# V and its ones columns stored at a pitch of 200 columns instead of 194

## Chip, cores, metric

One core of one Trainium2 chip. The metric is device time in microseconds (us) of one execution.

## The reference

Two branches share one normalised input: sliding-block attention over the last 512 keys of a cache (32 heads of 192), and a gated feed-forward net. Only the attention matters here (condensed; xn is the normalised input):

```python
W = min(4096, max(256, Sk // 4))                      # 512 keys
q = (xn @ wq).reshape(B, Sq, Hq, Dh).transpose(0, 2, 1, 3)
v = v_cache[:, :, Sk - W:, :]
p = softmax(einsum("bhqd,bhkd->bhqk", q, k) * Dh ** -0.5)
o = einsum("bhqk,bhkd->bhqd", p, v)                   # the product that reads V
...
return x + (o_rows @ wo) * silu(ffn(xn))
```

Sizes: 2048 queries, model width 640, Dh = 192, bf16.

## The kernel before

V of two heads lies in one tile: 128 keys on the partitions, then 4 key chunks (kc), 2 heads (h), and 192 columns of V followed by two columns of ones. The product with the unnormalised softmax weights reads 193 of these columns, so that column 192 of the result is the sum of the weights, by which `divide` divides.

```python
V_p = consts.tile([P, KC, 2, Dh + 2], bf, name="V_p")          # pitch 194 columns, 388 bytes
...
nc.gpsimd.memset(V_p[:, :, :, Dh : Dh + 2], 1.0)               # once
...
def load_v(pr):                                                # L121, once for each pair of heads
    for h in range(2):
        nc.sync.dma_start(out=V_p[:, :, h, 0:Dh], in_=vv[2 * pr + h, k0:Sk, :]. ... )
...
# in pv, line 487, for all pairs of heads but the last two: two row tiles of 64 keys, side by side
for kc in range(KC):
    for n, r in enumerate((lo, hi)):
        ...
        m = nc.tensor.matmul(
            acc[:, k, h * 256 : h * 256 + Dh + 1],
            Ps[i][kc][r, h, qt * P : (qt + 1) * P], V_p[r, kc, h, 0 : Dh + 1], ...)
...
# in pv_full, line 539, the last two pairs: all 128 keys at once
nc.tensor.matmul(acc[:, k, h * 256 : h * 256 + Dh + 1],
                 Ps[i][kc][:, h, qt * P : (qt + 1) * P], V_p[:, kc, h, 0 : Dh + 1], ...)
```

A "slice" below is one (kc, h) of V_p, the moving operand of one such matmul. `Ps`, the stationary operand, is the p_t of the profile. The slices are read in the order h=0, kc 0 to 3, then h=1, kc 0 to 3. (In L487 the two row tiles of a slice start mostly 19 or 20 ns apart and run side by side; they are called a pair, and count once.)

The softmax here doesn't subtract the row's maximum and nothing guards it: scores larger than these inputs give would overflow.

## Time and profile before

| | before |
|---|---|
| time, median of 3 runs | 920.98 us (920.84 to 921.37) |
| span of the profiled run | 919.1 us |
| TensorE busy | 914.2 us, 99% |
| next busiest engine (VectorE) | 601.8 us, 65% |
| matmuls that read V_p | L487: 3584 (1792 pairs); L539: 256 |

The lines themselves stand in the prediction. The gaps from start to start on which it rests come from the single start times in the trace's records; a timeline, which merges neighbours, shows only sums of such gaps. The ends of matmuls, and so their durations, are modelled in this profile and not measured.

The view of the instructions that touch V_p gives durations as minimum/median/maximum:

```profile
L487 PE MATMUL mm<-V_p,p_t x3520: 241/242/244, 190.4 to 817.2; 64*128 64x193 bf16 x196
L539 PE MATMUL mm<-V_p,p_t x224: 244/246/258, 841.3 to 900.4; 128*128 128x193 bf16 x112
```

### The profile page before, as it was taken

To read this page: it belongs to the slowest core of one execution; us is meant where nothing else is said; L and a number is where in the kernel's file an instruction comes from. 1 tells how busy PE (TensorE), PEld (TensorE's weight loads), DVE (VectorE), ACT (ScalarE), POOL (GpSimd) and SP (SyncE) were. 2 spreads that over 40 slices of the span, in tenths; PEclk is the share of its full clock that TensorE was granted. 3 is DMA by queue.
4 is the path that set the end of the run, shared out by engine and by line. 5 is a ranking of instruction groups with operands and counts; after the bars stand their busy time and mean duration, and the time that the engine had idled before them with its cause. 6 is when DMAs were issued, how large, how long until landed. Compare 5 with 4: busy or idle time off the path is not lost.

```text
span 919.1 us, 23174 instructions
## 1 busy us (share of the span) xinstructions
PE 914.2 (99%) x9920; PEld 548.9 (60%) x9920; DVE 601.8 (65%) x844; ACT 473.9 (52%) x840; POOL 85.2 (9%) x269
## 2 busy tenths in 40 slices
PE   9999999999999999999999999999999999999998
PEld 6444444465757575656565656566666666665665
DVE  6443321467677777777777777676867777777657
ACT  4222222557464646565656565655555555556471
POOL 0000000000000000000000000000000000001976
PEclk9999999999999999999999999999999999999999
DMA  9412430045352534253534343435243444443525
GB/s 299 79 35 64 92 82 0 1 75 112 54 113 50 111 51 108 54 108 54 108 58 109 57 108 52 110 53 108 56 87 73 90 77 75 91 71 102 120 59 166
DMA packets 248167, 77.53 MB, mean 84 GB/s; under 512 B 228993, under 2 KB 248065, under 8 KB 248065
## 3 DMA queue, kind: packets, MB, share of 16 engines
q1 hardware_dynamic: 245696, 73.39, 38.9%
q10 hardware_dynamic: 2368, 2.67, 0.9%
q8 instruction: 77, 1.26, 0.6%
q14 instruction: 26, 0.20, 0.1%
HBM read 38.93 MB, written 2.62 MB: 45 GB/s over the span
## 4 chain that ended last, share of the span: by engine, by line
PE 99%; DMA 1%; DVE 0%; ACTq 0%; issue 0%
PE mm L448 22%; PE sc L462 18%; PE mm L487 16%; PE sc L602 15%; PE sc L282 11%; PE mm L312 6%; PE sc L572 4%; PE sc L564 2%; PE mm L539 2%; PE mm L564 1%; DMA x_t<-in_A_x_dram 1%; PE gu L282 0%; PE mm L321 0%; PE sc L487 0%; PE sc L539 0%; PE mm L462 0%
## 5 line engine op out<-in xcount | busy, mean ns | idle before, releaser
L466 ACT ACTIVATE p_t<-sc 128x1024 bf16<-128x1024 f32 x254 | 252.9, 1022 | 120.5 <-PE sc L462 120.5
L453 DVE TENSOR_REDUCE qT<-mm 128x512 bf16<-128x1024 f32 x189 | 231.1, 1223 | 99.0 <-PE mm L448 96.5
L517 ACT ACTIVATE O_b<-mm,r 128x192 bf16<-128x192 f32 x486 | 164.6, 421 | 183.7 <-issue 136.9
L448 PE MATMUL mm<-xnT,wq_p 64*128 64x512 bf16 x1890 | 237.5, 376 | 0.0
L462 PE MATMUL sc<-qT,khat 64*128 64x512 bf16 x1524 | 198.0, 376 | 0.0
L487 PEld LDWEIGHTS <-p_t 64*128 64x128 bf16 x3584 | 159.3, 93 | 33.8
L487 PE MATMUL mm<-V_p,p_t 64*128 64x193 bf16 x3520 | 176.7, 242 | 0.0
L615 DVE TENSOR_TENSOR s_m<-s_m,sc 128x1024 f32<-128x1024 f32 x108 | 131.9, 1221 | 60.7 <-PE sc L602 52.3
L602 PE MATMUL sc<-wo_p,OT_b 64*128 64x512 bf16 x1296 | 168.8, 376 | 0.0
L448 PEld LDWEIGHTS <-wq_p 64*128 64x128 bf16 x1890 | 105.0, 94 | 98.9 <-issue 0.8
L462 PEld LDWEIGHTS <-khat 64*128 64x128 bf16 x1536 | 85.3, 94 | 80.4 <-DVE s_t L615 0.3
L602 PEld LDWEIGHTS <-OT_b 64*128 64x128 bf16 x1296 | 70.1, 94 | 44.1 <-issue 0.3
L615 DVE TENSOR_TENSOR s_t<-s_t,sc 128x512 f32<-128x512 f32 x108 | 74.2, 687 | 28.4 <-PE sc L572 26.6
L589 POOL MEMSET turn_t<- 128x1 f32 x220 | 21.6, 98 | 700.2 <-PE mm L487 506.2
L290 DVE TENSOR_TENSOR hT<-sc,sg 128x512 bf16<-128x512 f32 x46 | 31.7, 692 | 81.5 <-ACT sg L289 81.5
L289 ACT ACTIVATE sg<-sc 128x512 bf16<-128x512 f32 x46 | 27.3, 596 | 69.8 <-PE sc L282 69.8
L282 PE MATMUL sc<-xnT,wu_sb 128*128 128x512 bf16 (+1 forms) x260 | 60.5, 355 | 0.0
L282 PE MATMUL sc<-xnT,wg_sb 128*128 128x512 bf16 (+1 forms) x260 | 60.3, 355 | 0.1
L572 PE MATMUL sc<-OT_b,wo_p 64*128 64x512 bf16 (+1 forms) x345 | 50.3, 376 | 0.0
L312 PE MATMUL mm<-wd_sb,hT 128*128 128x512 bf16 x192 | 43.9, 379 | 0.0
L282 PEld LDWEIGHTS <-wu_sb 128*128 128x128 bf16 x285 | 27.2, 98 | 26.8 <-issue 0.2
L282 PEld LDWEIGHTS <-wg_sb 128*128 128x128 bf16 x285 | 27.2, 98 | 26.3
(83 smaller groups left out, 418.8 us busy)
## 6 DMA issues: line engine op xcount, KB each, us to landing
wo_p<-in_A_wo_dram SPq DMA_DIRECT2D x16, 480.0 KB, 4.8
K_p<-in_A_k_cache_dram SPq DMA_DIRECT2D x32, 192.0 KB, 4.6
V_p<-in_A_v_cache_dram SPq DMA_DIRECT2D x32, 192.0 KB, 3.6
wq_p<-in_A_wq_dram SPq DMA_DIRECT2D x64, 80.0 KB, 2.9
wq_p<-in_A_wq_dram SPq DMA_DIRECT2D x16, 160.0 KB, 3.2
x_t<-in_A_x_dram SPq DMA_DIRECT2D x13, 160.0 KB, 3.2
x_b<-in_A_x_dram SPq DMA_DIRECT2D x4, 512.0 KB, 6.4
OT_b<-O_b SPq DMA_TRANSPOSE x124, 2.8
```

Source lines behind the costliest of these rows:

```text
L282: nc.tensor.matmul(out, w_sb[:, c, f * P : (f + 1) * P], xnT[:, c, qc], start=(c == 0), stop=(c == NC - 1),)
L290: nc.vector.tensor_tensor(hTs[b][:, f, :], u, sg[:], ALU.mult)
L312: nc.tensor.matmul(dn, at, by, start=(f == 0), stop=(f == NF - 1))
L448: nc.tensor.matmul(q_ps[:, h, :], pairs[pr]["wq"][r, c, j * P : (j + 1) * P], xnT[r, c, b * 512 : (b + 1) * 512], start=(c == 0), stop=(c ...
L453: nc.vector.reduce_sum(qTs[i][:, j, :], q_ps[:, :, :].rearrange("p h n -> p n h"), axis=AX.X)
L462: nc.tensor.matmul(sc[:, h, :], khat[r, j, ks], qT[r, j, :], start=(j == 0), stop=(j == 2))
L466: nc.scalar.activation(p_t[:, :, :], sc[:, :, :], ACT.Exp, scale=scale)
L487: m = nc.tensor.matmul(acc[:, k, h * 256 : h * 256 + Dh + 1], Ps[i][kc][r, h, qt * P : (qt + 1) * P], V_p[r, kc, h, 0 : Dh + 1], start=(p ...
L517: nc.scalar.activation(O_b[:, qt, h, :], a_k[:, h, 0:Dh], ACT.Copy, scale=r[:, k, h, :])
L572: nc.tensor.matmul(ps.rearrange("p (t q) -> p t q", q=P), pairs[i // NB]["wo"][r, j, MC:D], OTs[i][:, :, :].rearrange("p (t j) q -> p j t ...
L602: m = nc.tensor.matmul(ps[:, k, :], OTs[i][r, 3 * (2 * half + k) + j, :], pairs[i // NB]["wo"][r, j, MAIN], start=(turn == 0 and j == 0), ...
L615: nc.vector.tensor_tensor(to, to, ps, ALU.add)
```

## The change

The intent: 194 columns are 388 bytes, so slices begin at 0, 4, 8 or 12 bytes past a multiple of 16. With 200 columns, 400 bytes, each begins at a multiple of 16. It was hoped that TensorE would then read V faster.

```diff
-    V_p = consts.tile([P, KC, 2, Dh + 2], bf, name="V_p")
+    V_p = consts.tile([P, KC, 2, Dh + 8], bf, name="V_p")
```

What else moves with it is told in the prediction.

## The prediction

> **What bounds the kernel now.** I read the page from the top: busy shares, then the chain that ended last, then the costliest groups, then the DMA issues.
>
> ```profile
> PE 914.2 (99%) x9920; PEld 548.9 (60%) x9920; DVE 601.8 (65%) x844; ACT 473.9 (52%) x840; POOL 85.2 (9%) x269
> ...
> PE 99%; DMA 1%; DVE 0%; ACTq 0%; issue 0%
> ```
>
> Only TensorE matters: it is busy 914.2 of 919.1 us and makes up 99% of the chain; the next engine is at 65%. The granted clock is 9 tenths or more in all 40 slices. Whatever shortens the stream of matmuls shortens the kernel by as much, and a change elsewhere must first use up a third of the span.
>
> ```profile
> L448 PE MATMUL mm<-xnT,wq_p 64*128 64x512 bf16 x1890 | 237.5, 376 | 0.0
> L487 PEld LDWEIGHTS <-p_t 64*128 64x128 bf16 x3584 | 159.3, 93 | 33.8
> L487 PE MATMUL mm<-V_p,p_t 64*128 64x193 bf16 x3520 | 176.7, 242 | 0.0
> ...
> V_p<-in_A_v_cache_dram SPq DMA_DIRECT2D x32, 192.0 KB, 3.6
> ```
>
> These are groups and one DMA row of the page. The number after the bar is busy time, then the mean of one, then idle time before it. V_p is read by L487 only as the moving operand (193 columns: 192 of V and one of ones), and no idle time stands before it. The same groups with shapes kept apart show the other reader of V_p, the last pair of heads:
>
> ```profile
> L539 PE MATMUL mm<-V_p,p_t 128*128 128x193 bf16 x224 | 20.8, 246 | 0.0
> ...
> L539 PE MATMUL sc<-V_p,p_t 128*128 128x193 bf16 x32 | 2.8, 246 | 0.0
> ```
>
> The duration of one matmul (242 ns) is not its cost, as matmuls overlap. What each takes from the span is the time to the next start. The timeline of a stretch shows it:
>
> ```profile
> 515.25 0.85 PE L487 MATMUL mm<-V_p,p_t 64*128 64x193 bf16 x16
> 515.92 1.47 PE L602 MATMUL sc<-wo_p,OT_b 64*128 64x512 bf16 x12
> 517.22 0.85 PE L487 MATMUL mm<-V_p,p_t 64*128 64x193 bf16 x16
> ```
>
> The first column is the start. Sixteen matmuls of L487 take 515.92 - 515.25 = 0.67 us. They run in pairs, rows 0 to 63 beside rows 64 to 127, so that is 8 pairs at 84 ns. The twelve of L602 take 1.30 us, 6 pairs at 217 ns.
>
> The single start times in the trace's records are finer, and they decide this prediction. I took the gap from each L487 pair to whatever starts next and sorted the 1792 pairs by slice of V_p. With h the head and kc the key chunk, a slice starts at (2 kc + h) x 388 bytes. In the order of execution, mean gaps in ns are: h=0: 83.1, **85.8**, 82.5, 82.5; h=1: 82.5, **86.7**, 82.5, 82.5. Each is a mean over 224 pairs. The slow two are kc=1. They repeat to within 1 ns (85 or 86; 86 or 87), whatever rows of p_t are the weights and whatever stretch of the kernel. L539, not row-tiled and in another order of heads and query tiles, has the same pattern: 85.8 and 86.7 at kc=1, and 82.5 elsewhere except 83.5 for the first. The first slice's 83.1 comes from following a 512-column matmul (83.3 there, 82.5 after another L487), so it is not the address's.
>
> [...]
>
> **The change part by part.** No instruction is added, removed or reordered. Three things move.
>
> First, slice starts go from multiples of 388 bytes to multiples of 400. The kernel before, as built, has V_p at byte 16,896, a multiple of 64, and everything in front of it stays. Before, starts modulo 32 are 0, 8, 16, 24 for kc 0 to 3 of h=0 and 4, 12, 20, 28 for h=1: eight different values, of which 8 and 12 are slow. Afterwards they are 0 for all of h=0 and 16 for all of h=1. Both values occur before, at kc=0 and kc=2 of h=0, and both cost 82.5 ns. I chose the modulus 32: 16 fails, as 8 and 12 modulo 16 also occur at kc=3, which is fast. If the address causes the slow slices, then all pairs should take 82.5. The gain in L487 is 224 x (85.83 - 82.50) + 224 x (86.67 - 82.50) = 0.75 + 0.93 = 1.68 us. In L539, with 32 matmuls for each slice, it is 32 x (3.28 + 4.22) = 0.24 us. All of it lies on the path, as TensorE has nothing to wait for. Sum: -1.92 us, 0.2%.
>
> Second, V_p grows by 8 slices x 6 columns x 2 bytes = 96 bytes per partition, so every buffer placed behind it moves by 96 bytes: xnT, khat, qT, wq_p, p_t and OT_b from 32 to 0 modulo 64. [...]
>
> Third, the V loads write rows of 384 bytes at a 400-byte pitch, and the ones columns are set at another pitch, once. The 32 loads land in 3.6 us median; the table of waits has no wait of TensorE for V_p, so a faster or slower landing is hidden: 0. The set of ones is one 113 ns instruction at the very start: 0.
>
> Full effect: 920.98 - 1.92 = 919.06 us. My point value is a mixture of this and no gain, below.
>
> **The rivals.** *Nothing happens* (921.0 us). The slow slices come from the position in the sequence and not the address. For it: [...]the ends of matmuls are more even than their starts (durations 241 to 244 ns, longer just where the gap is longer), so the records may only shift a start within an even 83.5 ns pace. Against it: kc=2 is the same kind of matmul as kc=1, and h=0 and h=1 differ though the sequence is the same.
>
> *The new starts hit slow places* (922.9 us). Modulo 64 the new starts are 0, 16, 32 and 48; the last two don't occur before. If they are slow, four of eight slices cost some 3.75 ns extra instead of two, so 256 x 4 x 3.75 = 3.84 us of excess in place of 1.92. Nothing in the trace suggests it beyond two slow values out of eight.
>
> *Alignment frees more* (down to 914.6 us). If the whole overhead of V_p's matmuls were due to alignment they would go at 193/2.4 = 80.4 ns: 149.7 + 21.4 us of gaps now against 2048 x 80.4 = 164.7, 6.4 us less. Against it: the first slice, which starts at a multiple of 64 bytes already, costs 82.5, and 512-column matmuls from 32-byte-aligned buffers carry the same small overhead.
>
> *The 96-byte shift moves something else*, such as a transposing DMA or a ScalarE write. ScalarE and VectorE have 48% and 35% of the span free, so I allow 0.5 us either way.
>
> **Range and chances.** I give 0.55 to the full gain (919.1), 0.25 to nothing (921.0), 0.08 to slow places, 0.05 to more, and the rest to shifts. The mean is 919.7; I lean to the likeliest outcome and say 919.4. Three runs before lie within 0.5 us. The range is 918.5 to 921.4. Even the largest rival is 0.7%, so "within 2%" is nearly certain: 0.98, and 0.01 for each side.
>
> **What would show it.** Right: gaps of L487 pairs of 82.5 ns in all eight slices but for the first after a 512-column matmul, durations of L487 closer together than 241 to 244, L487 plus L539 taking 1.9 us less of the span, counts of instructions unchanged, and 512-column gaps still 215.8. Wrong at the first step: kc=1 still 3 to 4 ns slow, with the time at 921, or another slice slow. Wrong at the second: PV gaps as predicted but other groups changed. A new wait of TensorE for V_p, or a clock below full, would make the whole prediction wrong.

The forecast's sum is -1.92 us (1.68 in L487 and 0.24 in L539). One term of 0 is that for the buffers moved by 96 bytes; in the trace before, pairs of their 512-column matmuls start 215.7 to 216.0 ns apart (means of L448, L462 and L602).

The 2.4 in the rival "Alignment frees more" is columns per ns. The trace before shows it: in L564, 256 columns take 109.2 ns from start to start and 512 take 215.7, 0.416 ns for each further column. The 80.4 ns and the 914.6 us are an estimate from that price. The "small overhead" is 82.5 ns against 80.4, and 215.8 ns for 512 columns against 512/2.4 = 213.3.

## The result, and the profile after

| | before | after |
|---|---|---|
| time, median of 4 runs | 921.0 us (920.84 to 921.37) | 920.5 us (920.35 to 921.18) |
| ratio | | 0.9995, 95% interval 0.9978 to 1.0013 |
| span of the profiled run | 919.1 us | 919.1 us |

A ratio is always the mean time of one kernel's runs over that of the other's of the same rounds, so it isn't quite the ratio of the medians quoted.

The page of the kernel after, its engines and its chain:

```profile
PE 912.6 (99%) x9898; PEld 548.9 (60%) x9920; DVE 601.7 (65%) x844; ACT 474.4 (52%) x840; POOL 85.3 (9%) x269
...
PE 99%; DMA 1%; DVE 0%; ACTq 0%; issue 0%
```

The bound is unchanged. TensorE's 1.6 us less busy time is no gain: 22 matmul records are missing from this trace (9898 of 9920), all of them outside the groups that read V_p. (The repeat of this kernel, number 1 below, has all 9920 and shows 913.8 us.)

The V load did land faster, 3.3 us against 3.6 (but the K load, whose tile kept its pitch, also went from 4.6 to 4.4), and nobody waits for it:

```profile
V_p<-in_A_v_cache_dram SPq DMA_DIRECT2D x32, 192.0 KB, 3.3
```

The instructions that touch V_p, kernel after:

```profile
L487 PE MATMUL mm<-V_p,p_t x3520: 243/243/243, 190.6 to 817.2; 64*128 64x193 bf16 x196
L539 PE MATMUL mm<-V_p,p_t x224: 247/247/257, 841.3 to 900.4; 128*128 128x193 bf16 x112
```

All L487 durations are now the same, 243 ns. The gaps became as even, but not as the prediction had it. Mean gap in ns from the start of an L487 pair to the next start, by slice, from the start times in the records:

```
            h=0: kc 0   1     2     3     h=1: kc 0   1     2     3     sum of L487, us
before        83.12 85.83 82.50 82.50       82.50 86.67 82.50 82.50     149.66
after         83.35 83.32 83.33 83.35       83.32 83.33 83.35 83.32     149.33
```

The two slow slices lost 2.5 and 3.3 ns, and the others gained 0.8 ns, all but the first one. Every slice now costs 83.33 ns, or 200 clocks. (A clock here is 0.417 ns, the price of one more column in these traces: from 192 columns, 82.5 ns in number 6, to 512 columns, 215.8 ns, it is 133.3 ns for 320 columns. Turned round, it is the 2.4 GHz of a forecast below.) L487 gained 0.33 us and L539 0.04 us. L602 and L572, the matmuls after the last slices, took 0.09 and 0.05 us more. From the first L448 of the attention to the last matmul it is 748.26 us before and 748.05 us after: 0.2 us, where 1.9 was expected. (There is one trace of the kernel before. Number 2, which reads V_p in the same way, comes to within 0.03 us of its stretch, when its four stray gaps are taken off.)

The timeline of the stretch that the prediction showed, kernel after (start, length):

```profile
515.36 0.85 PE L487 MATMUL mm<-V_p,p_t 64*128 64x193 bf16 x16
516.02 1.47 PE L602 MATMUL sc<-wo_p,OT_b 64*128 64x512 bf16 x12
517.32 0.76 PE L487 MATMUL mm<-V_p,p_t 64*128 64x193 bf16 x14
```

Eight pairs take 516.02 - 515.36 = 0.66 us, against 0.67 before; at this resolution the change can't be seen.

Before this stretch lies the feed-forward net, up to the first L448. It took 167.03 us in the trace before and 167.23 after, and between 166.77 and 168.05 over all 14 traces. Those 1.3 us from start to start are larger than the whole effect, so the traces decide here and the times only bound it.

### The profile page after: what moved, and what is told of

Same layout as the page of the kernel before. It is cut to its first block, busy times and chain, and to the rows that moved or that the text cites. A ratio compares the mean times of both kernels' runs of the same rounds, so it can differ in the third digit from the quotient of the medians.

```text
span 919.1 us, 23152 instructions
## 1 busy us (share of the span) xinstructions
PE 912.6 (99%) x9898; PEld 548.9 (60%) x9920; DVE 601.7 (65%) x844; ACT 474.4 (52%) x840; POOL 85.3 (9%) x269
## 4 chain that ended last, share of the span: by engine, by line
PE 99%; DMA 1%; DVE 0%; ACTq 0%; issue 0%
PE mm L448 22%; PE sc L462 18%; PE mm L487 16%; PE sc L602 15%; PE sc L282 11%; PE mm L312 6%; PE sc L572 4%; PE sc L564 2%; PE mm L539 2%; PE mm L564 1%; DMA x_t<-in_A_x_dram 1%; PE gu L282 0%; PE mm L321 0%; PE sc L539 0%; PE sc L487 0%
## 5 line engine op out<-in xcount | busy, mean ns | idle before, releaser
L448 PE MATMUL mm<-xnT,wq_p 64*128 64x512 bf16 x1890 | 237.5, 376 | 0.0
L462 PE MATMUL sc<-qT,khat 64*128 64x512 bf16 x1524 | 198.0, 376 | 0.0
L487 PEld LDWEIGHTS <-p_t 64*128 64x128 bf16 x3584 | 159.0, 94 | 33.8
L487 PE MATMUL mm<-V_p,p_t 64*128 64x193 bf16 x3520 | 176.4, 243 | 0.0
L602 PE MATMUL sc<-wo_p,OT_b 64*128 64x512 bf16 x1296 | 168.9, 376 | 0.0
L448 PEld LDWEIGHTS <-wq_p 64*128 64x128 bf16 x1890 | 105.0, 94 | 98.9 <-issue 0.8
L462 PEld LDWEIGHTS <-khat 64*128 64x128 bf16 x1536 | 85.3, 94 | 80.4 <-DVE s_t L615 0.3
L602 PEld LDWEIGHTS <-OT_b 64*128 64x128 bf16 x1296 | 70.3, 94 | 44.1 <-issue 0.3
L572 PE MATMUL sc<-OT_b,wo_p 64*128 64x512 bf16 (+1 forms) x345 | 50.3, 376 | 0.0
```

The source lines that it names most:

```text
L448: nc.tensor.matmul(q_ps[:, h, :], pairs[pr]["wq"][r, c, j * P : (j + 1) * P], xnT[r, c, b * 512 : (b + 1) * 512], start=(c == 0), stop=(c ...
L462: nc.tensor.matmul(sc[:, h, :], khat[r, j, ks], qT[r, j, :], start=(j == 0), stop=(j == 2))
L487: m = nc.tensor.matmul(acc[:, k, h * 256 : h * 256 + Dh + 1], Ps[i][kc][r, h, qt * P : (qt + 1) * P], V_p[r, kc, h, 0 : Dh + 1], start=(p ...
L572: nc.tensor.matmul(ps.rearrange("p (t q) -> p t q", q=P), pairs[i // NB]["wo"][r, j, MC:D], OTs[i][:, :, :].rearrange("p (t j) q -> p j t ...
L602: m = nc.tensor.matmul(ps[:, k, :], OTs[i][r, 3 * (2 * half + k) + j, :], pairs[i // NB]["wo"][r, j, MAIN], start=(turn == 0 and j == 0), ...
```

## The experiments

What was open: why did the slices at 82.5 ns get slower when they were aligned? Three theories were set against each other.

- *Even pace*: a slice of 193 columns costs 200 clocks, 83.33 ns, wherever it starts. A different offset only shifts the recorded start of a matmul within that pace.
- *Slow places*, the prediction's: starts at 8 or 12 modulo 32 cost 3 to 4 ns more, the true cost elsewhere is 82.5 ns, and something else, such as the shift of the other buffers, gave the gain back.
- *Groups of eight*: the 200 clocks of the kernel after are also 25 x 8, so the price could go by groups of eight columns, 25 of them for 193 columns as for 200. This was a guess; nothing but that one number spoke for it.

Three batches of four kernels ran, each of five rounds with the kernel before on the same chip (medians of the kernel before 921.29, 921.04 and 921.25 us). The edits of numbers 2, 5 and 8 are shown against the kernel before, those of the others against the changed kernel. "Stretch" is the time from the first L448 to the first L539, from the start times: 674.28 us in the kernel before. It holds all 1792 pairs of L487 and excludes the unsteady beginning.

### 1. The changed kernel again

No edit.

> The changed kernel again, in five rounds. Even pace (each pair takes 200 clocks of 2.4 GHz, 83.33 ns, wherever its slice starts; the offset only shifts the recorded start): all eight slices 83.3 ns again, durations all 243 ns, and the whole 0.3 to 0.5 us below the kernel before, ratio 0.9995. Slow places removed but given back elsewhere: the same gaps, time anywhere within 0.5 us.

Measured: 921.03 us, ratio 0.9994 (0.9982 to 1.0007). Gaps of 83.3 ns in all slices, durations 243 ns, L487 149.34 us, stretch 674.10 us, as in the first trace of this kernel. The trace's numbers repeat to 0.01 us; the times can't tell the kernels apart.

### 2. The shift of the other buffers alone

```diff
     V_p = consts.tile([P, KC, 2, Dh + 2], bf, name="V_p")
+    pad_t = consts.tile([P, 48], bf, name="pad_t")
+    nc.gpsimd.memset(pad_t[:], 0.0)
```

> Pitch 194 as before, with a 96-byte tile behind V_p, so that all later buffers stand where the change puts them. Even pace: the pattern of before stays (85.8 and 86.7 ns at kc=1, 82.5 elsewhere), L487 gaps sum to 149.7 us, time as before, 921.0. If the shift of the other buffers is what slowed the 82.5 ns slices to 83.3 in the changed kernel: slices at 83.3 with kc=1 at 86.7 and 87.5, sum of L487 and L539 1.7 us more, time 922.7.

Measured: 922.09 us, ratio 1.0005 (0.9992 to 1.0017). The gaps are those of before: 85.85 and 86.69 ns at kc=1, 82.5 elsewhere, but for the first slice (83.0) and the last (84.06). The last's mean holds four single gaps of 149 to 216 ns, 0.35 us more than four of 82.5. Each of them ends 155 ns after GpSimd began to write `turn_t` (line 591 of this kernel), so TensorE seems to have waited for that write; the profile names it in one of the four, and why it happens in this build only is open. Without the excess L487 sums to 149.64 us, as before (149.66). So the shift alone did not slow the 82.5 ns slices; the new pattern came with the pitch. The median was 0.8 us above that of the kernel before, between the two forecasts, so the time alone would not have told them apart. In its trace, which is of a slower run (922.58 us), 1.0 us more than in the trace before lies ahead of the attention (168.05 us to the first L448), where V_p isn't read.

### 3. Pitch 200, every slice 8 bytes late

```diff
-                out=V_p[:, :, h, 0:Dh],
+                out=V_p[:, :, h, 4 : 4 + Dh],
-        nc.gpsimd.memset(V_p[:, :, :, Dh : Dh + 2], 1.0)
+        nc.gpsimd.memset(V_p[:, :, :, 4 + Dh : 6 + Dh], 1.0)
...            # and in both matmuls
-                        V_p[r, kc, h, 0 : Dh + 1]
+                        V_p[r, kc, h, 4 : Dh + 5]
```

> Pitch 200, but every slice starts 8 bytes into its 400 bytes, so at 8 modulo 16 (8 modulo 32 for h=0, 24 for h=1). Even pace: flat 83.3 ns, sum of L487 149.3 us, time as the changed kernel, 920.5. A start at 8 modulo 32 costs 85.8 ns (the prediction's reading): h=0 at 85.8, h=1 at 82.5, sum over 2048 matmuls 172.4 us against 170.7 of the changed kernel, time 922.2.

Measured: 921.17 us, ratio 0.9999 (0.9986 to 1.0011). Flat 83.3 ns, durations 243 ns, L487 149.34 us, stretch 674.10 us: the numbers of the changed kernel, with no slice at a multiple of 16 bytes. The slow place at 8 modulo 32 is refuted: h=0 starts there in every slice and is not slow. The other one, 12, isn't tried here; in number 8 the slice h=0, kc=3 starts at 12 modulo 32 and has a gap of 82.49 ns (a single gap, so only a hint).

### 4. 200 columns instead of 193

```diff
-                        acc[:, k, h * 256 : h * 256 + Dh + 1],
+                        acc[:, k, h * 256 : h * 256 + 200],
-                        V_p[r, kc, h, 0 : Dh + 1]
+                        V_p[r, kc, h, 0 : 200]
...            # in both matmuls; eight ones columns are set
```

> As the changed kernel, but 200 columns read instead of 193 (eight ones columns; result unchanged). Cost goes by columns (N + 6 clocks, rounded up to an even number): 206 clocks, 85.83 ns, 2048 x 2.5 ns = 5.1 us more, 925.6 us. [...]

(The answer of groups of eight: 83.3 ns, as the changed kernel.)

Measured: 925.98 us, ratio 1.0052 (1.0039 to 1.0066). Every slice at 85.83 ns, 206 clocks. Groups of eight as the only price is refuted: 200 columns are 25 groups too and cost 2.5 ns more than 193. The run also tests what the prediction took for granted, that such nanoseconds lie on the path: stretch and tail (first L539 to the last matmul) grew by 4.46 + 0.64 = 5.10 us over the changed kernel, and 2048 x 2.5 ns is 5.1 us; the median is 4.95 us above number 1's.

The timeline of this kernel:

```profile
517.46 0.87 PE L487 MATMUL mm<-V_p,p_t 64*128 64x200 bf16 x16
518.14 1.04 PE L602 MATMUL sc<-wo_p,OT_b 64*128 64x512 bf16 x8
```

Eight pairs take 0.68 us, against 0.66 in the changed kernel.

### 5. Pitch 194, everything 16 bytes later

```diff
-    V_p = consts.tile([P, KC, 2, Dh + 2], bf, name="V_p")
+    V_f = consts.tile([P, 8 + KC * 2 * (Dh + 2)], bf, name="V_p")
+    V_p = V_f[:, 8:].rearrange("p (k h d) -> p k h d", k=KC, h=2)
```

> Pitch 194 as before, but V_p begins 16 bytes later, so the starts modulo 32 are 16, 24, 0, 8 for h=0 and 20, 28, 4, 12 for h=1. If the recorded start goes by the absolute address modulo 32 (slow at 8 and 12), the long gaps move from kc=1 to kc=3: 85.8 and 86.7 ns there. If they come from the sequence of offsets or of instructions, they stay at kc=1. Either way, with an even pace the sum of L487 stays within 0.3 us of 149.7 and the time at that of before.

Measured: 922.11 us, ratio 1.0006 (0.9993 to 1.0018). Neither answer came out: the long gaps are spread. One slice has sometimes 82 or 83 ns and sometimes 85 to 87. Means are 83.11, 85.05, 82.51, 83.69 for h=0 and 82.51, 84.93, 82.51, 85.56 for h=1. Where a group of eight follows another such group, the long gaps sit mostly at kc=3, as the absolute address modulo 32 would have it (means of 85.3 and 86.2 ns there and 83.0 at kc=1, over the 60 such groups); after other matmuls they sit at kc=1 and, for h=1, often at kc=3 as well. So the recorded start depends on the address and on what ran before. The pace hardly changes: L487 150.05 us, stretch 674.46 us. That is 0.39 and 0.18 us more than before; the sum was expected within 0.3.

### 6. 192 columns (a wrong result)

```diff
-                        V_p[r, kc, h, 0 : Dh + 1]
+                        V_p[r, kc, h, 8 : 200]
...            # in both matmuls; 192 columns of output, the sum now in column 184
```

> Pitch 200, 192 columns read (8 to 199: without the first eight of V, with eight ones), a wrong result on purpose. Even pace by columns: 192 + 6 = 198 clocks, 82.5 ns in every slice, 2048 x 0.83 = 1.7 us below the changed kernel, 919.2. If the 82.5 ns of before were the true cost of an odd 193 columns, 192 should go lower still, 82.1 ns or less.

Measured: the result is wrong, as intended; 919.72 us, ratio 0.9982 (0.9969 to 0.9995). Every slice at 82.5 ns, 198 clocks; L487 147.84 us, stretch 672.62 us. With the tail, 0.21 us shorter, the trace lost the 1.7 us expected; the time, 0.5 us over its forecast, is less sharp. So 82.5 ns is what 192 columns cost, and the gaps of 82.5 ns in the kernel before are no price of 193 columns (number 10 shows the same by its sum).

### 7. 194 columns

```diff
-                        V_p[r, kc, h, 0 : Dh + 1]
+                        V_p[r, kc, h, 0 : 194]
...            # in both matmuls
```

> Pitch 200, 194 columns read, result unchanged. Column count rounded up to even plus 6: 200 clocks, 83.3 ns, the same as 193 columns, time as the changed kernel within 0.3 us. Without such rounding: 0.4 ns more for each pair, 0.85 us more.

Measured: 920.59 us, ratio 0.9994 (0.9981 to 1.0006). 83.3 ns in every slice, stretch 674.10 us: exactly as 193 columns. In these runs columns come in twos: 192 cost 198 clocks (82.5 ns), 193 and 194 cost 200 (83.33 ns), 200 cost 206 (85.83 ns), and 512 (in L448 and others) cost 518 (215.8 ns). Each is the column count, rounded up to an even number, plus 6; 193 is the only odd count among them.

### 8. Pitch 193

```diff
-    V_p = consts.tile([P, KC, 2, Dh + 2], bf, name="V_p")
+    V_p = consts.tile([P, KC, 2, Dh + 1], bf, name="V_p")
-        nc.gpsimd.memset(V_p[:, :, :, Dh : Dh + 2], 1.0)
+        nc.gpsimd.memset(V_p[:, :, :, Dh : Dh + 1], 1.0)
```

> Pitch 193 columns, 386 bytes: worst alignment, starts at 0, 4, 8, 12 modulo 32 for h=0 and 2, 6, 10, 14 for h=1, so every second slice starts off a 4-byte boundary. Even pace: single gaps of 82.5 to 87 ns in some pattern, mean over the eight 83.3 to 83.6, time 921 within 0.5 us. If misalignment costs what the prediction thought: three or more slices at 85.8 or above, mean above 84.5, 2 us or more on the time.

Measured: 921.88 us, ratio 1.0007 (0.9994 to 1.0021). Gaps from 82.5 to 87 ns in a pattern that again depends on what ran before; mean 83.83 ns, a little over the range expected; L487 150.22 us, stretch 674.84 us. Such starts do cost something: the stretch is 0.74 us over the changed kernel's and 0.56 us over that of the kernel before, whose starts are all at multiples of 4. The time, expected within 0.5 us of 921, was 0.88 over it. An even pace wherever a slice starts is therefore too simple, and the last four runs look for what is charged.

### 9. Pitch 200, every slice 2 bytes late

As number 3, with 1 column in place of 4.

> Pitch 200, every slice starts 2 bytes into its 400 bytes: 2 modulo 16, off a 4-byte boundary, all eight alike. If only a change of offset modulo 16 from one slice to the next costs: flat 83.3 ns, durations all alike, L487 149.3 us, 920.5 us. If misalignment itself costs: more than 83.5 ns in every slice.

Measured: 922.61 us, ratio 1.0015 (1.0003 to 1.0028). Flat, but at 84.17 ns, 202 clocks (the first slice 83.56); L487 150.69 us, stretch 675.58 us, 1.49 us over the changed kernel. Misalignment itself costs here, one step of two clocks for each slice. The instructions that touch V_p in this run:

```profile
L487 PE MATMUL mm<-V_p,p_t x3520: 243/245/245, 190.4 to 818.5; 64*128 64x193 bf16 x196
```

The durations are nearly all 245 ns, where the changed kernel has 243.

### 10. Pitch 196

```diff
-    V_p = consts.tile([P, KC, 2, Dh + 8], bf, name="V_p")
+    V_p = consts.tile([P, KC, 2, Dh + 4], bf, name="V_p")
```

> Pitch 196: kc steps of 784 bytes keep the offset modulo 16 (0 for h=0, 8 for h=1), only the step from head to head changes it by 8. If only a change modulo 16 counts: 83.3 ns within a head, at most two gaps off it at the head switches, L487 between 149.3 and 149.6 us. If a change modulo 32 counts too (kc alternates between 0 and 16): a mixture of 82.5 and 85 to 87 ns as before.

Measured: 921.25 us, ratio 1.0001 (0.9988 to 1.0015). Gaps of h=0: 83.3 ns four times. Gaps of h=1: 85.82, 82.51, 82.49, 82.51, which again make 4 x 83.33. (Of these, kc=0 and kc=2 both start at 8 modulo 32, and only one has a long gap.) L487 149.34 us, stretch 674.10 us: the changed kernel's total, with single gaps shaped like those of before. This is the even pace at its plainest: the records of three slices show 82.5 and one shows 85.8, and nothing is lost or gained. My expectation of at most two odd gaps, at the head switches, was wrong in its detail. The tile is 64 bytes smaller than with pitch 200. The instructions that touch V_p, with uneven durations again:

```profile
L487 PE MATMUL mm<-V_p,p_t x3520: 241/243/243, 190.5 to 817.1; 64*128 64x193 bf16 x196
```

### 11. 194 columns, every slice 14 bytes late

```diff
-    V_p = consts.tile([P, KC, 2, Dh + 8], bf, name="V_p")
+    V_f = consts.tile([P, KC * 2 * (Dh + 8) + 8], bf, name="V_p")
+    V_p = V_f[:, 7 : 7 + KC * 2 * (Dh + 8)].rearrange("p (k h d) -> p k h d", k=KC, h=2)
...            # 194 columns in both matmuls; the whole tile set to ones; to make room, a small constant was taken out
```

> 194 columns from 14 bytes into each 400-byte slice: [...] Cost by columns: flat 83.3 ns as there, 920.5 us. [...]

("There" is number 7. The guess of groups of eight: 194 columns that begin 7 columns into a group would be 26 groups, 208 clocks, 86.7 ns.)

Measured: 925.29 us, ratio 1.0046 (1.0033 to 1.0059). Most gaps are 85.83 ns, 206 clocks, against 200 for the same 194 columns from an aligned start (number 7); stretch 678.20 us, 4.10 us more. Neither forecast was met: not flat 83.3, and not 86.7. So this start costs about as much as six more columns; what it pays for, this run can't say. The timeline of this run, whose lines have numbers one lower:

```profile
517.56 0.86 PE L486 MATMUL mm<-V_p,p_t 64*128 64x194 bf16 x16
518.25 1.04 PE L601 MATMUL sc<-wo_p,OT_b 64*128 64x512 bf16 x8
```

and of number 7, aligned:

```profile
515.04 0.85 PE L487 MATMUL mm<-V_p,p_t 64*128 64x194 bf16 x16
515.70 1.47 PE L602 MATMUL sc<-wo_p,OT_b 64*128 64x512 bf16 x12
```

0.69 us against 0.66 us for the same eight pairs of 194 columns.

### 12. Multiples of 8 bytes, stepping by 8 from chunk to chunk

```diff
-    V_p = consts.tile([P, KC, 2, Dh + 8], bf, name="V_p")
+    V_f = consts.tile([P, KC, 2 * (Dh + 8) + 4], bf, name="V_p")
+    V_p = V_f[:, :, 0 : 2 * (Dh + 8)].rearrange("p k (h d) -> p k h d", h=2)
...            # to make room, the same small constant was taken out as in number 11
```

> Head pitch 400 bytes, key-chunk pitch 808 bytes: all starts at a multiple of 8 bytes, but each kc steps by 8 modulo 16. If a change of offset counts: the uneven pattern of before (82.5 and 85 to 87 ns) in both heads, durations 241 to 244, L487 149.5 to 150.2 us. If the 4-byte starts of the kernel before made it: flat 83.3, 149.3 us.

Measured: 921.44 us, ratio 1.0005 (0.9992 to 1.0017). The pattern of before is back in both heads: 83.12, 85.79, 82.54, 82.48 and 82.54, 85.81, 82.48, 82.63 ns. So a change of offset from slice to slice makes the pattern, without any start at an odd multiple of 4. Yet the stretch is 674.10 us, the changed kernel's to 0.01 us, so it costs nothing. (L487 alone is 0.16 us more, 149.50 us, which L572 and L602 behind it give back.) The durations are 241 to 244 ns, as this forecast had them:

```profile
L486 PE MATMUL mm<-V_p,p_t x3520: 241/242/244, 191.2 to 817.9; 64*128 64x193 bf16 x196
```

### All runs together

| kernel | starts, bytes modulo 16 | columns | L487, us | stretch, us |
|---|---|---|---|---|
| before | 0, 4, 8, 12 | 193 | 149.66 | 674.28 |
| after; its repeat (1) | 0 | 193 | 149.33; 149.34 | 674.10; 674.10 |
| 8 bytes late (3) | 8 | 193 | 149.34 | 674.10 |
| pitch 196 (10) | 0, 8 | 193 | 149.34 | 674.10 |
| chunk step 8 (12) | 0, 8 | 193 | 149.50 | 674.10 |
| 194 columns (7) | 0 | 194 | 149.33 | 674.10 |
| 16 bytes later (5) | 0, 4, 8, 12 | 193 | 150.05 | 674.46 |
| pitch 193 (8) | every even number | 193 | 150.22 | 674.84 |
| 2 bytes late (9) | 2 | 193 | 150.69 | 675.58 |
| 192 columns (6) | 0 | 192 | 147.84 | 672.62 |
| 200 columns (4) | 0 | 200 | 153.81 | 678.56 |
| 14 bytes late (11) | 14 | 194 | 153.86 | 678.20 |

Starts at a multiple of 8 bytes, in the mixtures tried, give one and the same stretch. Starts at odd multiples of 4 among them cost 0.2 to 0.4 us in all, and off 4 bytes 0.7 us and more. Shift alone (2) is left out for its four stray gaps.

Put on one group of eight slices (224 in the stretch), the excess over the changed kernel is 0.83 ns, 2 clocks, before, 1.6 ns in number 5, 3.3 ns, 8 clocks, in number 8 and 6.6 ns, 16 clocks, in number 9. So 8 and 9 agree on two clocks for each slice that starts off a 4-byte boundary: four of the eight in number 8, all in number 9. This was read off after the runs and not tested by one. It leaves open why starts at odd multiples of 4 cost 2 clocks for each group before, about 4 in number 5 and nothing that can be seen in number 8, and what number 11 pays for. It isn't groups of eight columns alone: 25 of them cost 85.83 ns in number 4 and 83.33 in number 7. No correct version tried was clear of the changed kernel, so there is nothing faster to show.

## Why the prediction was right, and where it was wrong

**The bound: right.** TensorE stayed at 99% of the chain, no wait of TensorE for V_p came up (the trace after has one new wait, 0.5 us in line 335, long before V_p is read), and number 4 shows nanoseconds of a V_p slice arriving in the span one for one (2048 x 2.5 ns is 5.1 us; the trace grew by 5.10 us, the median by 4.95).

**The failed step: "If the address causes the slow slices, then all pairs should take 82.5."** The evenness came, at 83.33. The prediction read 82.5 ns as the cost of a good slice and the rest of the long gaps as excess. Numbers 6 and 7 show that 82.5 ns is the price of 192 columns, and 193 and 194 both cost 83.33. The short gaps in the kernel before were the other side of the long ones: a start recorded 6 or 8 clocks late makes the gap before it long (85.83 or 86.67 ns), and the gaps after it are each 2 clocks short of 83.33 (82.5). Whether the start itself or only its record is late, these traces can't say. Numbers 10 and 12 show the same shape with no loss at all. So nearly all that the prediction took for excess was none: the gain of 1.68 us in L487 shrank to 0.33 and the 0.24 us in L539 to 0.04; after what L602 and L572 lost, 0.2 us is left. Of the signs it named, durations closer together than 241 to 244 ns came (243); 82.5 ns in all eight slices and 1.9 us less in L487 and L539 did not (83.33 ns; 0.37 us).

**The modulus 32: wrong as a cost.** Number 3 starts half of the slices at 8 modulo 32 without harm, number 10 shows a long and a short gap at the same 8 modulo 32, and number 5 did not carry the slow slices over cleanly.

**The rival that came true** is "nothing happens", in the reason that the records "may only shift a start within an even 83.5 ns pace". The evidence stood in the prediction and was given 0.25. Gap plus difference of durations would have pointed to it before any run, though not proved it, as the ends are modelled: start plus duration, the end, moves on by 83.2 to 83.9 ns for every slice of the kernel before, long gap or not. What the rival took for the cause, that position in the sequence and not the address makes the pattern, fell: the pattern vanished with another pitch (gaps of 83.32 to 83.35 ns at pitch 200).

**Counted as nothing, and nothing:** the 96-byte shift (number 2 leaves the gaps as they were, and L448 takes 203.98 us in the traces before and after), the faster landing of V, the ones columns. (The growth of 96 bytes fitted, as the kernel after was built and ran.)

**The range held** (920.5 in 918.5 to 921.4), because the mixture kept weight on no gain. The point, 919.4, leaned to the step that failed. A range that takes in both outcomes, from runs that differ by 0.5 us among themselves, can't confirm the mechanism: that it held is no merit of the main argument.

**A slip of reading:** L539 is the last two pairs of heads, not the last one as the prediction has it; its counts are right.

## What to carry to other kernels

Take a difference of a few ns between start-to-start gaps for a cost only after checking that the sum over a whole cycle (or, as a hint, the modelled ends) differs as well; here recorded starts slipped within a constant pace. For slices like these (bf16 moving operand, 193 contiguous columns; other shapes were hardly tried) multiples of 8 bytes were enough: 16 gave nothing beyond 8 (stretch 674.10 us in numbers 1 and 3), and 4 lost at most 0.4 us of 920. Before paying memory for alignment, price the whole of it: here everything between the pace before (149.66 us for 1792 pairs) and the aligned one came to 0.3 us.
